# Late constants of a fused attention and mixture-of-experts kernel: one block of memsets on VectorE, or separately planned pieces

## The chip, the cores and the metric

The kernel runs on one core of one Trainium2 chip (the experiments ran in four sets, each on another such chip; a ratio always compares runs of one set). The metric is the device time of one execution in microseconds (us).

A word on names: PE is the matmul engine (TensorE), DVE is VectorE, ACT is ScalarE, POOL is GpSimd.

## The reference

Four batches of eight attention heads (768 tokens, head size 64). Every query sees its near neighbours (a band of 16 to each side) and one summary per block of 32 keys. The result x, 3072 x 512, goes through a mixture of eight experts whose weights P come from eight rounds of Sinkhorn normalization.

```python
scores_l = where(|i - j| < 16, q @ k.T / 8, -1e9)
scores_s = q @ k_blockmax.T / 8 + log(32)
a = softmax(concat([scores_l, scores_s]))
x = a @ concat([v, v_blockmean])                    # 4 batches x 8 heads
P = sinkhorn(exp(x @ w_gate - max), rounds=8)       # rows, then columns, scaled
out = sum over e of P[:, e] * (relu(x @ w1[e]) @ w2[e])
```

## The kernel before

The kernel is emitted in an order that a small planner in its own source works out. Work is cut into units; each has an engine, an estimated cost, dependencies and a rank. The planner simulates the engines with these costs and, wherever several units could start next on an engine, takes the one of lowest rank. A unit cannot be interrupted. The instructions of all engines are emitted in exactly that order, with semaphores where one engine's work needs another's.

```python
# Plan.order(), cut: for each engine, the units that could start first (within 0.02 us); among them the lowest rank
t = max([t0, free.get(e, 0.0)] + [d.end + d.lag + (HOP if d.on != e else 0.0) for d in u.deps])
best.setdefault(e, []).append((t, u, cost))
...
t_min = min(t for t, _, _ in c)
t, u, cost = min((x for x in c if x[0] <= t_min + 0.02), key=lambda x: x[1].prio)
```

Heads are worked in pairs. The four pairs of the first batch are done in two halves (h = 0, 1), so that the first expert can start on half of the tokens. The other twelve pairs are done whole, and these need some constants: zeros in E_e, zeros and ones in V_e, and col_en for the Sinkhorn stage. They are set once, after the masks of the last first-half pair.

```python
def late_constants():
    for t in E_e:
        nc.vector.memset(t[64:128, :, :], 0.0)
    for t in V_e:
        nc.vector.memset(t[:], 0.0)
        nc.vector.memset(t[0:24, :, D:VD], 32.0 / XS)
        nc.vector.memset(t[32:56, :, VD + D:2 * VD], 32.0 / XS)
    nc.vector.memset(col_en, float(E) / float(N))

# pair_half(i, h, rank), cut: masks -> value products -> normalization -> transposes -> copy into xT
U["mk", i, h] = add("DVE", 0.78, masks_h, [U["X", i, h], ...], rank)
U["ss", i, h] = add("PE", 0.22, summaries, ...)
U["A", i, h]  = add("PE", 0.65, values_h, [U["mk", i, h], U["sx", i, h], U["Vs", i]], rank)
U["no", i, h] = add("DVE", 0.68, normalize, [U["A", i, h], ...], rank)
U["xt", i, h] = add("PE", 0.18, to_xT, [U["no", i, h]], rank)
U["x", i, h]  = add({"ACT": 0.46, "DVE": 0.5}, 0, x_out, [U["xt", i, h]], rank)

# the order of building, cut
for i in range(PB):
    pair_start(i, i)
    pair_half(i, 0, i)
add("DVE", 2.4, late_constants, [U["mk", PB - 1, 0]], 5.5)
expert0(0, [U["x", i, 0] for i in range(PB)])       # first expert: hidden layer 'hps', second layer 'yps'
for i in range(PB):
    pair_half(i, 1, 10 + i)
...                                                # batches 1 to 3, the rest of expert 0
# then a "bridge" into the Sinkhorn stage, then experts 1 to 7: the main loop, whose order is fixed
```

The softmax here doesn't subtract the row's maximum and nothing guards it: scores larger than these inputs give would overflow.

## Time and profile before

Median 679.09 us of three runs (679.05 to 679.47). The profiled execution was another one: it took 684.06 us, its span was 681.4.

The first part of the page of the kernel before gives busy time, share of the span and number of instructions of each engine. The part on the chain says which engine the work that ended last ran through.

```profile
PE 670.5 (98%) x5189; PEld 441.6 (65%) x5189; DVE 585.4 (86%) x1445; ACT 407.7 (60%) x788; POOL 125.9 (18%) x165
...
PE 92%; DVE 4%; DMA 1%; issue 1%; ACT 1%; POOL 1%; DVEq 0%; ACTq 0%
```

PE is busy for 98% of the span and holds 92% of the chain. The list of waits of PE alone (who waited for whom, total us, times, longest) from 20 us to the end has only three entries:

```profile
PE sink L1077 <- DVE csum_sb L1072: 0.9, 1, 0.9
PE tx L506 <- ACT es L430: 0.6, 1, 0.6
PE sg L323 <- ACT qT L196: 0.4, 1, 0.4
```

The timeline of VectorE at the block (columns: start, duration, engine, line, operation, what is written from what, shape, count; in brackets the idle time before and what ended it):

```profile
23.50 0.78 DVE L593 MEMSET Ee<- 64x384 uint32 x2
24.41 0.38 DVE L595 MEMSET Ve<- 128x390 uint32 x1
...
25.89 0.17 DVE L598 MEMSET col_en<- 128x128 f32 x1
26.36 0.20 DVE L498 RECIPROCAL rc<-av 128x6 f32<-128x6 f32 x1 [0.30 <-PE av L468]
```

From the first memset to the end of the last: 23.50 to 26.06 us, 2.56 us. The normalization (L498 and the line after it) follows and had to wait 0.30 us more for the value products of PE. The timeline of PE there:

```profile
23.62 1.91 PE L544 MATMUL idle<-zeros 128*128 128x512 bf16 x4
25.33 0.72 PE L468 MATMUL av<-vx,Eh 128*128 128x65 bf16 x16
...
27.18 0.39 PE L323 MATMUL sg<-qT,kT 64*128 64x160 bf16 x8 [0.40 <-ACT qT L196]
...
29.04 0.33 PE L506 MATMUL tx<-ident,xs 128*128 128x128 f16 x3 [0.58 <-ACT es L430]
...
29.62 1.47 PE L200 MATMUL hps<-xT,w 128*128 128x384 f16 x8
```

The value products of the last first-half pair are "av<-vx,Eh" at 25.33; the four "idle" matmuls ahead of them are filler that the planner puts into gaps; "tx" are the transposes into xT and "hps" the first hidden-layer matmuls. In the view by stretches (length, busy us and count of each engine, granted clock, DMA) the stage looks like this:

```profile
15.28:25.52 10.24, 10.24 (x104) 6.59 (x103) 8.11 (x22) 4.60 (x7) 7.68 (x10) 0.50 1.47 195
25.52:36.00 10.48, 9.50 (x164) 6.54 (x162) 6.80 (x21) 8.08 (x14) 5.49 (x8) 1.00 1.98 172
```

The number after the POOL column is the granted clock: from 15.28 to 25.52 us PE ran at half its clock.

### The profile page before, as it was taken

How to read it: one execution, taken by the hardware profiler on the slowest of the kernel's cores; microseconds unless marked ns; L12 is line 12 of the kernel's file. 1: busy time of each engine (PE TensorE's matmuls, PEld its weight loads, DVE VectorE, ACT ScalarE, POOL GpSimd, SP SyncE). 2: the span in 40 equal slices, each digit the busy share in tenths (PEclk: the TensorE clock that was granted, in tenths of full speed). 3: DMA queues.
4: the chain of work that ended last, by engine and by line, in shares of the span. 5: the costliest groups of instructions: out<-in, count | busy, mean ns of one | idle time of the engine just before them, and what ended most of it. 6: DMA issues, size and time to landing. Idle time of an engine off the chain costs nothing.

```text
span 681.4 us, 13654 instructions
## 1 busy us (share of the span) xinstructions
PE 670.5 (98%) x5189; PEld 441.6 (65%) x5189; DVE 585.4 (86%) x1445; ACT 407.7 (60%) x788; POOL 125.9 (18%) x165
## 2 busy tenths in 40 slices
PE   8999999999999999999999999999999999999996
PEld 4665666545666666666666666666666666666665
DVE  6778898788599988999889988998899888998886
ACT  4677877656677765555555555555555555555551
POOL 8699630022202010100101010201010101100000
PEclk9799999999999999999999999999999999999999
DMA  9999990000503123310513050404131051301224
GB/s 120 188 143 143 98 144 7 1 1 0 78 1 37 12 31 48 31 17 1 78 17 33 1 78 1 48 1 60 19 31 17 7 72 17 32 1 48 78 93 155
DMA packets 113618, 33.90 MB, mean 50 GB/s; under 512 B 99984, under 2 KB 110736, under 8 KB 113552
## 3 DMA queue, kind: packets, MB, share of 16 engines
q0 software_dynamic: 104672, 26.22, 41.6%
q1 hardware_dynamic: 8352, 6.80, 3.3%
q8 instruction: 40, 0.66, 0.4%
q14 instruction: 26, 0.21, 0.1%
q10 hardware_dynamic: 528, 0.02, 0.0%
HBM read 52.45 MB, written 6.29 MB: 86 GB/s over the span
## 4 chain that ended last, share of the span: by engine, by line
PE 92%; DVE 4%; DMA 1%; issue 1%; ACT 1%; POOL 1%; DVEq 0%; ACTq 0%
PE xy L883 36%; PE pg L877 16%; PE pa L877 10%; PE pb L877 10%; PE yps L210 6%; PE hps L200 6%; PE sg L323 1%; PE tkq L304 1%; PE vs L331 1%; PE av L468 1%; PE tx L506 1%; DMA qst<-in_q_dram 1%; DVE out_acc L1018 1%; PE av L395 1%; PE av L401 1%
## 5 line engine op out<-in xcount | busy, mean ns | idle before, releaser
L883 PEld LDWEIGHTS <-hf 128*128 128x128 f16 x2352 | 230.1, 98 | 96.1 <-issue 1.2
L883 PE MATMUL xy<-w,hf 128*128 128x256 f16 x1312 | 183.4, 273 | 0.1
L883 PE MATMUL xy<-ws,hf 128*128 128x256 f16 x984 | 147.6, 273 | 0.1
L191 ACT ACTIVATE hf<-pg 128x512 f16<-128x512 f32 x84 | 50.2, 597 | 149.6 <-PE pg L877 149.4
L1018 DVE SCALAR_TENSOR_TENSOR out_acc<-xy,P_sb,out_acc 128x512 f32<-128x512 f32 x164 | 115.1, 744 | 1.7 <-PE xy L883 1.7
L824 DVE TENSOR_TENSOR hf<-hf 128x512 f16<-128x512 f16 x252 | 99.6, 422 | 8.8
L877 PE MATMUL pa<-xT,w 128*128 128x512 f16 x336 | 99.9, 379 | 0.0
L877 PEld LDWEIGHTS <-w 128*128 128x128 f16 x672 | 65.8, 98 | 43.6 <-issue 0.6
L827 DVE TENSOR_TENSOR hf<-pb,c 128x512 f16<-128x512 f32 x84 | 58.1, 692 | 38.2 <-PE pb L877 35.7
L176 POOL DMA_DIRECT2D w<-in_moe_w_dram x56 | 41.8, 759 | 220.3 <-PE pg L877 192.1
L877 PEld LDWEIGHTS <-ws 128*128 128x128 f16 x504 | 49.3, 98 | 25.3
L911 ACT COPY c<-pg 128x512 f32<-128x512 f32 x84 | 49.2, 585 | 22.7 <-PE pg L877 22.6
L827 DVE TENSOR_TENSOR hf<-pg,c 128x512 f16<-128x512 f32 x84 | 57.2, 681 | 0.6 <-PE pg L877 0.6
L191 ACT ACTIVATE hf<-pa 128x512 f16<-128x512 f32 x84 | 50.6, 603 | 0.4 <-PE pa L877 0.4
L896 ACT COPY pg<-pa 128x512 f32<-128x512 f32 x84 | 47.9, 570 | 4.8
L877 PE MATMUL pg<-xTs,w 128*128 128x512 f16 x168 | 50.0, 379 | 0.1
L877 PE MATMUL pb<-xT,ws 128*128 128x512 f16 x168 | 50.0, 379 | 0.0
L877 PE MATMUL pg<-xTs,ws 128*128 128x512 f16 x168 | 50.0, 379 | 0.0
L877 PE MATMUL pg<-xT,w 128*128 128x512 f16 x168 | 50.0, 379 | 0.0
L877 PE MATMUL pb<-xTs,ws 128*128 128x512 f16 x168 | 50.0, 379 | 0.0
L904 ACT COPY c<-pb 128x512 f32<-128x512 f32 x84 | 49.8, 593 | 0.2 <-ACT pg L896 0.2
L200 PE MATMUL hps<-xT,w 128*128 128x384 f16 x256 | 48.7, 326 | 0.0
(136 smaller groups left out, 842.5 us busy)
## 6 DMA issues: line engine op xcount, KB each, us to landing
w<-in_moe_w_dram POOLq DMA_DIRECT2D x8, 1024.0 KB, 9.3
w<-in_moe_w_dram POOLq DMA_DIRECT2D x56, 128.0 KB, 3.5
out_dram<-out_acc SPq DMA_DIRECT2D x22, 256.0 KB, 2.0
qst<-in_q_dram POOLq DMA_DIRECT2D x32, 96.0 KB, 5.8
vx<-in_v_dram POOLq DMA_DIRECT2D x16, 192.0 KB, 6.5
kst<-in_k_dram POOLq DMA_DIRECT2D x24, 96.0 KB, 6.0
w<-in_moe_w_dram POOLq DMA_DIRECT2D x2, 512.0 KB, 8.3
kst<-in_k_dram POOLq DMA_DIRECT2D x4, 192.0 KB, 4.9
```

The costliest lines, as they stand in the source:

```text
L176: nc.gpsimd.dma_start(out=t[:, :, h, :], in_=moe_w1[e].rearrange("(dk p) f -> p dk f", p=128)[:, :, f:f + 128])
L191: nc.scalar.activation(out=out, in_=in_, func=AF.Relu, bias=0.0, scale=1.0)
L200: nc.tensor.matmul(hp[:, 0:n], lhsT=w1s[e][:, dk, 128 * f:128 * (f + 1)], rhs=xT[:, dk, t0:t0 + n], start=(dk == 0), stop=(dk == KD - 1))
L210: nc.tensor.matmul(yp[:], lhsT=h[:, f, c * 128:(c + 1) * 128], rhs=w2s[e][:, f, :], start=(f == 0), stop=(f == KF - 1))
L824: nc.vector.tensor_tensor(out=out, in0=in0, in1=in1, op=ALU.subtract)
L827: nc.vector.tensor_tensor(out=out, in0=in0, in1=in1, op=ALU.add)
L877: nc.tensor.matmul(bank[:], lhsT=w[:, dk, :], rhs=x[:, dk, :], start=start and dk == 0, stop=dk == KH - 1, skip_group_check=True)
L883: nc.tensor.matmul(bank, lhsT=a(f)[:, 128 * c:128 * (c + 1)], rhs=w[:, f, :], start=start and f == 0, stop=f == FH - 1, skip_group_check=True)
L896: nc.scalar.copy(out=B["g"][:], in_=B["a"][:])
L904: nc.scalar.copy(out=B["c5"][:], in_=B["b"][:])
L911: nc.scalar.copy(out=B["c2"][:], in_=B["g"][:])
L1018: nc.vector.scalar_tensor_tensor(out=acc, in0=src, scalar=P_sb[:, t, e:e + 1], in1=acc, op0=ALU.mult, op1=ALU.add)
```

## The change

The intent: give the planner seven small units at a low rank in place of one block of 2.4 us, so that it may put more urgent VectorE work, such as the normalization, in between. (It was described as eight pieces; the code makes two for E_e, four for V_e and one for col_en.) The memsets themselves are the same nine.

```diff
         def late_constants():
-            for t in E_e:
-                nc.vector.memset(t[64:128, :, :], 0.0)
-            for t in V_e:
-                nc.vector.memset(t[:], 0.0)
+            def zero(t):
+                nc.vector.memset(t, 0.0)
+
+            def ones(t):
                 nc.vector.memset(t[0:24, :, D:VD], 32.0 / XS)
                 nc.vector.memset(t[32:56, :, VD + D:2 * VD], 32.0 / XS)
-            nc.vector.memset(col_en, float(E) / float(N))
+
+            parts = [(0.4, lambda t=t: zero(t[64:128, :, :])) for t in E_e]
+            for t in V_e:
+                parts += [(0.4, lambda t=t: zero(t[:])), (0.15, lambda t=t: ones(t))]
+            return parts + [(0.15, lambda: nc.vector.memset(col_en, float(E) / float(N)))]
...
-        add("DVE", 2.4, late_constants, [U["mk", PB - 1, 0]], 5.5)
+        c1 = U["mk", PB - 1, 0]
+        for us, fn in late_constants():
+            c1 = add("DVE", us, fn, [c1], 12.5)
```

## The prediction

> **What bounds the kernel now.** The tensor engine. The page shows PE busy 670.5 us of 681.4 (98%), and PE holds 92% of the chain that ended last. After 26 us the list of PE's waits has only three: 0.9 us for the Sinkhorn column sum (139 us), 0.6 us for an exponential's output (29.0 us) and 0.4 us for a copied query (27.2 us). The rest is matmul that this change doesn't touch, so there is little to win.
>
> **What the change does.** The same 9 memsets run on VectorE. In the timeline they are one run from 23.50 to 26.06 us: E_e 0.78, V_e 0.38 twice, four small ones 0.06 each, col_en 0.17; 2.56 us with the gaps. (The diff makes seven units of them, not eight.) Nothing is removed or added. What changes is the planner's view: instead of one 2.4 us block it has seven links of 0.15 to 0.4 us at a lower rank, so that other vector work may come between. In the plan the normalization of the last first-half pair can start about 1.2 us earlier (after three pieces, 1.2, for 2.4), and with it the transposes into xT, their copy, and the first expert's first matmuls.
>
> **What of it is critical.** On the chip the block is nearly free. From 15.3 to 25.5 us PE ran at a granted clock of 0.5 (windows view: 0.50 in 21 to 23.5). The last pair's value products therefore ran at 25.33 to 26.3, and VectorE, done with the block at 26.06, still waited 0.30 us for them. So the direct saving is about zero; after the change VectorE waits longer before that normalization, and the 1.2 us of constants left over go into its next gaps (27.15 to 28.34 is idle now). The gain can only come from PE's order after the value products: from 26.1 to 29.0 us PE is busy 1.96 of 2.90 us. If the last pair's xT is transposed earlier, the first hidden-layer matmuls (29.62 us now) can come about 1 us earlier and fill these holes. The plan is unchanged up to the block, so I expect the same first 23 us, filler matmuls and half-clock stage. Everything later is reshuffled a little, at PE full; that may win or lose some tenths of a us, also at the Sinkhorn stage.
>
> [...] I expect no second slow stage.
>
> **Prediction.** 678.4 us (0.7 less), 8 in 10 between 676.6 and 680.0. Faster by over 2%: 1%; within 2%: 98%; slower by over 2%: 1%.
>
> **What would show it.** The memsets stand in several places, mostly within 23.5 to 31 us, with a normalization between them; their busy sum stays about 2 us. The normalization still starts at 26.2 to 26.5 us and waits for PE. The first hidden-layer matmul starts at 28 to 29 us. PE's idle time between 26 and 30 us shrinks from 1.0 to under 0.5 us. PE's clock is 0.5 until 25.5 us and 1.0 after. From 30 us on the same work is shifted by under 1.5 us.
>
> **What would make it wrong.** A new order that delays a copy or mask of the second halves, so that PE waits where it is full today; constants so late that the neighbour-value transfers (first at 35.5 us) wait for them; a second half-clock window; or a Sinkhorn chain that starts later or meets the expert matmuls worse.

The sum: the median before, 679.1 us, less 0.7 for the earlier hidden layer, is 678.4.

## The result, and the profile after

| | runs | median us | range |
|---|---|---|---|
| before, first set | 4 | 679.28 | 679.05 to 679.72 |
| after, first set | 4 | 680.03 | 678.55 to 680.71 |
| before, second set | 11 | 679.58 | 679.18 to 682.60 |
| after, second set (a_copy) | 6 | 679.31 | 678.72 to 679.92 |

Ratio after to before: 1.0007 (95% interval 0.9989 to 1.0025) in the first set and 0.9990 (0.9974 to 1.0005) in the second. A ratio here is the mean time of one kernel's fast runs over that of the other's of the same rounds, so it is not quite the ratio of the medians in the table. The change moves the time by nothing that these runs can show. All outputs are right. My figure was 678.4 with a range of 676.6 to 680.0; the first median lies 0.03 us over its upper end, the second inside.

The first part of the page of after, then the list of PE's waits in after from 20 us on:

```profile
PE 667.0 (98%) x5189; PEld 438.4 (65%) x5189; DVE 583.2 (86%) x1445; ACT 406.1 (60%) x788; POOL 125.3 (18%) x165
```

```profile
PE pg L883 <- DVE xT L830: 0.8, 1, 0.8
PE ss L419 <- DVE xT L196: 0.5, 1, 0.5
PE sg L323 <- ACT qT L196: 0.4, 1, 0.4
PE tx L506 <- DVE xs L499: 0.2, 1, 0.2
```

The wait for the exponential (0.6 us, at 29.04 before) is gone, as hoped. But two new ones came, both for VectorE: 0.5 us for a copy of xT (at 70 us) and 0.8 us at the bridge into the Sinkhorn stage; the latter stands in place of the 0.9 us for the column sum. The timelines of VectorE and then of PE at the block in after, and its view by stretches:

```profile
22.23 0.79 DVE L593 MEMSET Ee<- 64x384 uint32 x2
23.14 0.38 DVE L593 MEMSET Ve<- 128x390 uint32 x1
23.56 0.20 DVE L498 RECIPROCAL rc<-av 128x6 f32<-128x6 f32 x1
...
24.62 0.38 DVE L593 MEMSET Ve<- 128x390 uint32 x1
...
25.33 0.17 DVE L602 MEMSET col_en<- 128x128 f32 x1
```

```profile
21.21 1.03 PE L544 MATMUL idle<-zeros 128*128 128x512 bf16 x4
22.08 0.64 PE L468 MATMUL av<-vx,Eh 128*128 128x65 bf16 x16
...
23.85 0.39 PE L323 MATMUL sg<-qT,kT 64*128 64x160 bf16 x8 [0.40 <-ACT qT L196]
24.40 0.34 PE L506 MATMUL tx<-ident,xs 128*128 128x128 f16 x3 [0.16 <-DVE xs L499]
24.67 0.50 PE L409 MATMUL ss<-qT,ksT 64*32 64x384 bf16 x4
...
25.56 0.82 PE L200 MATMUL hps<-xT,w 128*128 128x384 f16 x4
```

```profile
15.28:25.52 10.24, 8.55 (x152) 5.53 (x143) 8.81 (x28) 6.66 (x12) 7.53 (x10) 1.00 1.47 195
```

The order is the one that the planner was meant to find: three memsets, the normalization, six memsets; the transposes now stand ahead of the summary products "ss", and the hidden layer starts at 25.56. But everything is three microseconds earlier than in the trace of before, and that is not the change's doing. The code up to 22 us is the same in both kernels. The difference is the clock: 1.00 here, 0.50 there. The two profiles cannot be compared by their clock times. So I measure everything from one event: the start of the value products of the last first-half pair (25.33 before, 22.08 after), the last thing that is the same in all kernels (early_block below, which moves the block ahead of it, and the two with an extra ScalarE copy at the very start apart). From there to the end of the trace, before took 681.42 - 25.33 = 656.09 us, and after 678.06 - 22.08 = 655.98. I call this "the measure". Two traces of the same kernel agree in it within 0.11 us (before and b_copy, after and a_copy, plan_only and plan_only2), which is far better than the timed runs do, and it is the yardstick for the experiments. Most kernels have one trace only, so differences of about 0.1 us are not read.

### The profile page after: what moved, and what is told of

Read it like the earlier page. It is cut to its first block, busy times and chain, and to the rows that moved or that the text cites. A ratio compares the mean times of both kernels' runs of the same rounds, so it can differ in the third digit from the quotient of the medians.

```text
span 678.1 us, 13655 instructions
## 1 busy us (share of the span) xinstructions
PE 667.0 (98%) x5189; PEld 438.4 (65%) x5189; DVE 583.2 (86%) x1445; ACT 406.1 (60%) x788; POOL 125.3 (18%) x165
## 4 chain that ended last, share of the span: by engine, by line
PE 91%; DVE 5%; DMA 1%; POOL 1%; issue 1%; ACT 0%; DVEq 0%; POOLq 0%; ACTq 0%
PE xy L889 36%; PE pg L883 16%; PE pb L883 11%; PE pa L883 11%; PE yps L210 6%; PE hps L200 6%; PE tkq L304 1%; PE sg L323 1%; DMA vx<-in_v_dram 1%; DVE out_acc L1024 1%; PE vs L331 1%; PE tx L506 1%; PE av L395 1%; PE av L401 1%; PE ss L419 1%
```

## The experiments

My theory was that the change wins a few tenths at the block and that the new order behind it gives them back. The rivals: the block was never critical; or the difference lies in the clock of the runs. Numbers of all traces, in us. "To loop" is from the value products to the first second-layer matmul of the main loop ("xy"), "loop" from there to the end, and the measure is their sum (rounded each for itself).

| kernel | value products to normalization | to first "hps" | to loop | loop | measure | timed median (runs) | ratio to before |
|---|---|---|---|---|---|---|---|
| before, half clock to 25.5 | 1.03 | 4.29 | 150.99 | 505.10 | 656.09 | | |
| b_copy | 2.55 | 4.20 | 150.91 | 505.09 | 655.99 | 679.95 (6) | 1.0005 (0.9986 to 1.0023) |
| after | 1.48 | 3.48 | 151.24 | 504.74 | 655.98 | 680.03 (4) | 1.0007 (0.9989 to 1.0025) |
| a_copy | 1.43 | 3.43 | 151.21 | 504.66 | 655.87 | 679.31 (6) | 0.9990 (0.9974 to 1.0005) |
| dve_only | 1.48 | 3.58 | 150.91 | 505.10 | 656.01 | 680.53 (6) | 1.0022 (0.9997 to 1.0047) |
| plan_only | 2.74 | 4.75 | 152.52 | 504.65 | 657.18 | 682.15 (6) | 1.0030 (1.0013 to 1.0046) |
| plan_only2 | 2.74 | 4.75 | 152.51 | 504.66 | 657.17 | 683.09 (4) | 1.0041 (1.0011 to 1.0071) |
| local_only | 1.48 | 3.80 | 150.57 | 505.10 | 655.67 | 680.10 (4) | 1.0018 (0.9986 to 1.0051) |
| later_only | 2.75 | 4.19 | 151.62 | 504.66 | 656.28 | 679.63 (4) | 0.9999 (0.9978 to 1.0020) |
| early_block | 0.94 | 3.27 | 151.02 | 505.09 | 656.11 | 679.44 (4) | 1.0001 (0.9977 to 1.0025) |
| act_shift | 2.74 | 4.21 | 150.90 | 504.73 | 655.63 | 679.48 (6) | 0.9996 (0.9970 to 1.0023) |
| best | 1.48 | 3.80 | 150.56 | 504.66 | 655.23 | 679.46 (6) | 0.9990 (0.9969 to 1.0012) |
| fill | 2.75 | 4.75 | 152.51 | 504.68 | 657.19 | 680.66 (6) | 1.0005 (0.9984 to 1.0025) |
| copy_first, half clock to 25.0 | 1.17 | 3.48 | 151.26 | 504.68 | 655.94 | 680.65 (6) | 1.0007 (0.9990 to 1.0024) |

### b_copy and a_copy: the two kernels again

No edit.

> The kernel before again, for a trace at the full clock. Both theories: ratio 1.000. If the half-clock stage of the first profile (15.3 to 25.5 us, clock 0.992 over the span) belongs to the run and not to the kernel, this trace has none and its span is about 676 to 678 us. Theory 'locally won, given back later': at full clock the block of memsets (22.2 to 24.8 us) does hold up the normalization, which starts at 24.9 and not at 23.6 us as after, and the first hidden-layer matmul comes at 26.4 to 26.8 (25.56 after). Rival 'never critical': the first hidden-layer matmul starts within 0.3 us of 25.56.

> The changed kernel again: ratio 1.000 to 1.001, and its PE trace up to 36 us as in the first trace of it where the clock is the same.

In b_copy the half clock lasted 3.41 us (16.88 to 20.29), so this trace shows the block of before at full clock, here VectorE and then PE:

```profile
22.95 0.78 DVE L593 MEMSET Ee<- 64x384 uint32 x2
...
25.35 0.17 DVE L598 MEMSET col_en<- 128x128 f32 x1
25.54 0.20 DVE L498 RECIPROCAL rc<-av 128x6 f32<-128x6 f32 x1
```

```profile
23.00 0.63 PE L468 MATMUL av<-vx,Eh 128*128 128x65 bf16 x16
23.56 0.34 PE L468 MATMUL av<-Vs,es 64*128 64x130 bf16 x3
...
24.76 0.39 PE L323 MATMUL sg<-qT,kT 64*128 64x160 bf16 x8 [0.40 <-ACT qT L196]
...
26.61 0.33 PE L506 MATMUL tx<-ident,xs 128*128 128x128 f16 x3 [0.58 <-ACT es L430]
...
27.20 1.47 PE L200 MATMUL hps<-xT,w 128*128 128x384 f16 x8
```

Now VectorE is the late one: the value products end at about 23.9, and the normalization starts at 25.54, when the block is done. So the block does hold up the normalization, by about a microsecond against after (2.55 and 1.48 us behind the start of the value products). The half clock of the first profile had hidden this. What it costs PE is less: PE has other work, and its two idle stretches, 0.40 and 0.58 us, shrink to 0.40 and 0.16 after. Nor is it the late normalization alone that holds PE here: the profile puts the end of the 0.58 us down to ScalarE's exponential "es" (its first one ends at 26.57 us, the normalization at 26.33). In the trace of before the normalization was done 1.89 us ahead of the transposes "tx", and yet these stood 3.71 us behind the start of the value products, here 3.61. In dve_only below the same transposes start 2.98 us behind it and ahead of that exponential. How the order of VectorE brings the wait for the exponential about is not shown. The trace was not free of the stage and the span not 676 to 678 us, as I had hoped, and so the normalization and "hps" stand 0.4 to 0.8 us later by the clock than expected; relative to the value products the expectation of the first theory holds. The stage is also shorter than in the first trace of the same code (10.24 us): it belongs to the run and not to the kernel. a_copy showed no half clock, and its normalization and first "hps" stand as in the first trace of after; the ratio was 0.9990, just below the 1.000 to 1.001 expected.

### dve_only and plan_only: the two halves of the change apart

dve_only keeps the plan of before and moves only the memsets on VectorE; plan_only keeps the plan of after and puts the memsets back in one block.

```diff
# dve_only, against before
 def late_constants():                       # still one unit of 2.4 us in the plan
-    ...all nine memsets
+    ...E_e, E_e, V_e[0]; the other six go to a list
 def normalize(i, h):
     ...
+    while (i, h) == (PB - 1, 0) and rest:
+        rest.pop(0)()                       # behind the normalization of the last first-half pair
# plan_only, against after
-for us, fn in late_constants():
-    c1 = add("DVE", us, fn, [c1], 12.5)
+parts = late_constants()                    # same seven units in the plan; the first emits all nine memsets
+for n, (us, _) in enumerate(parts):
+    c1 = add("DVE", us, (lambda: [fn() for _, fn in parts]) if n == 0 else (lambda: None), [c1], 12.5)
```

> The order of all engines as before (planned with one block of 2.4 us), but on VectorE the normalization of the last first-half pair stands ahead of the last six memsets. If the block on the chip is what costs: the normalization starts at about 23.6 us and the time is 0.5 to 1.2 us shorter than before. If only the later order matters: same as before within 0.3 us.

> The order of all engines as after (planned in seven pieces), but the nine memsets stand in one block ahead of the normalization. If the block on the chip is what costs: 0.5 to 1.2 us longer than after, with a new wait of PE for the normalization (before the transposes into xT) near 24.5 to 25.5 us. If only the later order matters: same as after within 0.3 us.

plan_only shows what the block can cost (the timeline of PE). Its PE order asks for the transposes early, and they must wait for a normalization that stands behind the block:

```profile
23.77 0.39 PE L323 MATMUL sg<-qT,kT 64*128 64x160 bf16 x8 [0.41 <-ACT qT L196]
25.59 0.34 PE L506 MATMUL tx<-ident,xs 128*128 128x128 f16 x3 [1.42 <-DVE xs L499]
```

The line of 25.59 shows 1.42 us of idle PE ahead of the transposes, ended by the normalization ("xs"), and the measure is 1.20 us longer than after's 655.98, all of it still there at the end: what was lost at the block was not won back. dve_only, in turn, won 0.6 us up to the first "hps" and yet ended with the measure of before, which is the outcome "only the later order matters". Its trace shows where the gain went. At the first-layer matmuls just ahead of the transposes of pair 4's keys it was still 0.33 us ahead of b_copy (11.46 and 11.79 us behind the start of the value products), exactly where local_only below stands. Then the second of the two transfers of these keys landed 12.55 us after its issue, at 34.26 us (in b_copy 11.00 us after it, at 32.63), and the transposes of the keys started at 34.40 us, 0.34 us later behind those matmuls than in b_copy. (The profile names a copy of ScalarE for this wait, but in b_copy and local_only the same transposes start before that copy ends.) So a late transfer took the gain away. The edit doesn't touch this transfer, and no other trace was held up there; with one trace of dve_only, its measure decides nothing. The timed runs of plan_only were also slower than its trace explains, by more than a microsecond; more of that below.

### local_only, later_only, early_block: the block against everything behind it

local_only has the plan of before, with the order at the block (VectorE, and PE's transposes) made as after by hand. later_only has the plan of after, with the order at the block made as before. early_block moves the whole block to the start of the kernel.

```diff
# local_only, against dve_only
+for key in (("no", 3, 0), ("xt", 3, 0), ("x", 3, 0)):
+    place(U[key], ahead_of=U["ss", 0, 1])
# later_only, against plan_only
+for key in (("xt", 3, 0), ("x", 3, 0), ("S", 1, 1), ("X", 1, 1)):
+    place(U[key], ahead_of=U["hd", 0, 0])
# early_block, against before
-add("DVE", 2.4, late_constants, [U["mk", PB - 1, 0]], 5.5)
+add("DVE", 2.4, late_constants, [U["ident"]], -4.0)
```

> Planned as before (one block), and then by hand at the block only: the normalization ahead of the last six memsets, and the transposes and copy of the last first-half pair ahead of the summary products, as after has them. All other order is that of before. Measured from the start of the last pair's value products to the end of the trace, where the first 22 us (same code in all kernels) drop out: before 656.0 to 656.1 us, after 655.9 to 656.0. If the change wins locally and its later order gives the win back: 655.4 to 655.8. If the local order wins nothing that lasts: 655.9 to 656.2. In the timed runs under 0.2% either way.

> Planned as after (seven pieces), and then by hand at the block only: all nine memsets in one block ahead of the normalization, and the transposes, their copy and the next score products as before has them; the later order is that of after. Same measure. If the local order is worth about 0.3 us and the later order gives it back: 656.2 to 656.5. If the local order is worth nothing: 655.9 to 656.1.

> Before, with the whole block planned right behind the identity matrix (about 5.3 to 7.9 us) instead of at 22 us, so nothing stands between the value products and the normalization. If the block still costs something after the change: the normalization starts within 0.3 us of the end of its value products, and the measure from those products to the end is 655.2 to 655.8; the start may be up to 0.9 us later. If no place of the block matters: 655.9 to 656.2.

The two-by-two table of the measure comes out additive:

| measure, us | later order of before | later order of after |
|---|---|---|
| block as before | 655.99 (b_copy) | 656.28 (later_only) |
| block as after | 655.67 (local_only) | 655.98 (after) |

The order at the block (VectorE's and PE's together) is worth 0.32 us with the one later order and 0.30 with the other; act_shift and best below repeat the pair, with 0.40. The later order of after costs 0.29 and 0.31. The two cancel. The theory "won at the block, given back later" stands in the traces, and the rival "never critical" falls. The third, the clock of the runs, explains the spread of the timed runs: of the 46 runs of the code of before whose clock is on record, the 35 with a mean clock of 0.998 or more had spans of 677.0 to 678.6 us, the 8 with 0.995 or less 679.0 to 681.7. It also explains the look of the first profile, but hardly the measure: the half-clock stages reach only 0.19 us (before) and 0.59 us (copy_first) into it. (Both first traces also end at a clock of 0.5, before in its last 0.5 us and after in its last 0.2, but PE's last matmul has ended 5.5 us before the end in before and 5.6 in after.) The later cost has two parts with opposite signs, though: up to the main loop the later order of after loses 0.71 and 0.67 us (150.91 to 151.62, 150.57 to 151.24), and in the main loop it gains 0.43 and 0.36 (505.09 to 504.66, 505.10 to 504.74). The second is odd, because the order of the main loop is fixed and the same in all kernels.

The first is not what the list of waits suggests. The view by stretches from the value products to the loop, for b_copy, later_only, local_only and after (PE's busy time is the number behind the first comma):

```profile
23.00:173.91 150.91, 148.67 (x1491) 89.36 (x1490) 122.73 (x326) 105.29 (x178) 66.44 (x83) 1.00 0.99 75
21.68:173.30 151.62, 149.37 (x1491) 88.77 (x1491) 121.39 (x327) 103.78 (x178) 66.48 (x84) 1.00 0.98 76
21.62:172.19 150.57, 148.76 (x1490) 89.20 (x1490) 122.56 (x327) 105.20 (x178) 67.51 (x84) 1.00 0.99 77
22.08:173.32 151.24, 149.37 (x1490) 88.70 (x1490) 121.09 (x327) 103.90 (x178) 66.71 (x84) 1.00 0.99 75
```

PE is idle for 2.24 and 2.25 us with the block as before, for 1.81 and 1.87 us with the block as after: the order at the block wins 0.4 us of idle time, and the later order loses next to none. Its new waits (0.5 and 0.8 us) only take the place of others. Its loss of 0.71 and 0.67 us is nearly all in time in which PE is recorded as busy, 0.70 and 0.61 us more for as many matmuls. The profile's page says of itself that the ends of matmuls are modelled, so short stalls may hide in this time; whether they do, and what they are, is not shown.

early_block is the best at the block: the normalization follows the value products at once, and "hps" starts 0.2 us earlier than after. Its measure, 656.11, is that of before all the same: this is the outcome "no place of the block matters". But its own plan has a new later order too, with the same two later waits as after, so it is no clean test of the block. Against after it is 0.22 us shorter up to the loop (151.02 and 151.24) and 0.35 longer in it (505.09 and 504.74), and the second belongs to the effect of the next section. The start was not delayed either (value products at 21.63 us). The 0.2 to 0.8 us that I expected if the block still cost something are not there. In the timed runs none of these three differs from before.

### act_shift, best: the 0.4 us in the main loop

In traces with a loop of 505.1 us, PE is about 0.2 us late twice with a second-layer matmul, at 34.5 and 259.6 us behind the start of the loop; in the others it isn't. In both places ScalarE starts one copy ("c<-pg") 0.28 us later than in the other traces, although PE's product that it reads stands at the same time behind the start of the loop in both, and the two copies are 384 recorded ScalarE instructions apart. In every trace where the first of these copies is late, 319 recorded ScalarE instructions stand ahead of it, those that only wait for a semaphore or issue a transfer counted (before, b_copy, dve_only, local_only, early_block); where it is on time there are 320 (after, a_copy, the plan_only kernels) or 318 (later_only). The new plan swaps some copies and other work between ScalarE and VectorE, but as many of ScalarE's computing instructions stand ahead of the copy in after as in before (244); the number differs by one semaphore instruction. early_block has nearly the ScalarE work of after, but 319, and is late. So I shifted ScalarE's instruction stream by one:

```diff
# act_shift, against before; best, against local_only
 nc.scalar.activation(out=warm[:], in_=warm[:], func=AF.Exp, bias=0.0, scale=1.0)
+nc.scalar.copy(out=warm[:], in_=warm[:])     # 8 numbers, at the start, where ScalarE is idle
```

> Before, with one extra ScalarE copy of 8 numbers right at the start, so that every later ScalarE instruction has a number one higher. In all traces with the later order of before, ScalarE starts one copy 0.28 us late at two places of the main loop, 384 of its instructions apart, and PE loses 0.21 us at each; the traces with the later order of after, whose numbers are shifted by one or whose instruction there is another, do not. If it hangs on the number in the instruction stream: from the first second-layer matmul to the end 504.66 us instead of 505.10, and from the value products to the end 655.55 to 655.7. If it hangs on what the plan left behind on VectorE or in the buffers: 505.10 again.

> local_only and that extra copy: the local order of after, the later order of before, no late ScalarE copies. If both effects stand and add up: 655.2 to 655.3 us from the value products to the end, the shortest of all, 0.7 to 0.8 less than before and after. In the timed runs 0.1% at most, inside their spread. If the shift does nothing: 655.67 again.

The timelines of ScalarE, then of PE, at the first of the two places in b_copy:

```profile
207.00 0.59 ACT L911 COPY c<-pg 128x512 f32<-128x512 f32 x1 [0.56 <-PE pg L877]
```

```profile
207.77 0.59 PE L877 MATMUL pg<-xT,w 128*128 128x512 f16 x2
208.42 0.60 PE L883 MATMUL xy<-w,hf 128*128 128x256 f16 x4
```

The same instructions in act_shift:

```profile
205.44 0.58 ACT L912 COPY c<-pg 128x512 f32<-128x512 f32 x1 [0.28 <-PE pg L878]
```

```profile
206.49 0.59 PE L878 MATMUL pg<-xT,w 128*128 128x512 f16 x2
206.92 0.60 PE L884 MATMUL xy<-w,hf 128*128 128x256 f16 x4
```

The idle time of ScalarE ahead of the copy falls from 0.56 to 0.28 us, and the step from "pg" to "xy" on PE from 0.65 to 0.43. Loop: 504.73 instead of 505.09. In all 14 traces (act_shift and best have 320) the copy is late exactly where 319 instructions stand ahead of it, and one extra instruction, far away and without any use, puts it on time. So this part of the gain is not a merit of the change's order: it hangs on where an instruction stands in ScalarE's stream, or on something else that shifts with it, which was not tested apart. Why ScalarE is late there stays open; no record in the trace names it.

best puts local_only and the shift together: 655.23, the shortest measure, 0.76 us below before and 0.75 below after, as the sum of the two effects (655.99 - 0.32 - 0.36 = 655.31, an estimate from b_copy, local_only and act_shift) asks. In the timed runs it is 0.9990 of before, interval 0.9969 to 1.0012: not told apart from it.

### plan_only2 and fill: times that the trace does not explain

```diff
# fill, against plan_only
+if u is U["xt", PB - 1, 0]:
+    keep_busy(4)                            # four filler matmuls where PE stalls 1.4 us
```

> plan_only again. Its trace lost 1.2 us against after, its timed runs 2.8. If the block alone costs 1.2 us and the rest is half-clock windows that its longer stall of PE (1.4 us) brings on, another profile may show a window of 0.5 after 24 us, and the time is 681 to 683 us again. If the rest was chance: 680 to 681 us.

> plan_only with four filler matmuls in the stall of PE (1.4 us) ahead of the transposes; at full clock they take 0.86 us and fit in. The trace should not change: 657.1 to 657.3 from the value products to the end. If the timed runs of plan_only are 2.8 to 3.8 us slower, and not 1.2, because its stall brings on half-clock windows: now 680.3 to 681 us. If it is something else: 682 to 684 again.

plan_only2 is plan_only once more: the trace is the same within 0.01 us, again without a half-clock stage, and the timed runs are slow again (680.30, 683.71, 682.47, 683.89). With the filler the trace stays the same too (657.19), but the times fall to 679.99 to 681.15, which is what 1.2 us on top of before predicts. So 1.6 and 2.8 us of plan_only's loss (medians, each over the before of its own set) went away with four filler matmuls in the stall. (In the trace of plan_only, at a clock of 1.00, PE's next matmul starts 0.86 us behind the first of four such, at 22.00 and 21.14 us: the figure of the expectation.) That fits half-clock stages in the unprofiled runs. No kept trace of plan_only caught one, but the record has the mean clock of every timed run: 0.995 or 0.996 in the five unprofiled runs of plan_only and 0.993 to 0.996 in the three of plan_only2, against 0.998 in the two profiled ones, and 0.998 to 1.000 in all six runs of fill. So the slow runs did run at a lower clock, and with the filler none did. That the stall itself brings the lower clock on was my guess; these clocks fit it, no trace shows it. Where in these runs the half clock lay is not shown either.

### copy_first: the wait at 70 us

The wait that after shows at 70 us stands in the traces of after, a_copy, later_only, plan_only, fill and early_block, and in none with the later order of before. VectorE does a mask there before the copy that frees the buffer. So I took the copy first:

```diff
# copy_first, against after
+seq.remove(U["x", 7])
+seq.insert(seq.index(U["mk", 8, 0]), U["x", 7])
```

> After, with one change of order on VectorE at 69 us: the copy of pair 7 into xT ahead of the mask of pair 8, so that the buffer for which PE waits 0.50 us at 70.06 us (in every trace with the later order of after, in none of before) comes free 0.5 us sooner. All else is the order of after. If that wait is most of the 0.67 us that the later order costs ahead of the main loop: from the value products to the first second-layer matmul 150.6 to 150.8 us instead of 151.2, and to the end 655.3 to 655.5. If the mask, now later, makes PE wait as long, or the gain is lost at the Sinkhorn stage: 151.1 to 151.3 and 655.9 to 656.0.

The timeline of PE in after, then in copy_first, where the summary products stand:

```profile
70.06 0.65 PE L419 MATMUL ss<-qT,ksT 64*32 64x384 bf16 x4 [0.50 <-DVE xT L196]
```

```profile
72.17 0.34 PE L419 MATMUL ss<-qT,ksT 64*32 64x384 bf16 x2 [0.31 <-DVE xT L196]
72.67 0.34 PE L419 MATMUL ss<-qT,ksT 64*32 64x384 bf16 x2 [0.16 <-ACT kT L196]
```

The 0.50 us became 0.31 and 0.16: freed sooner from VectorE, PE waited for ScalarE instead. The measure is unchanged, 655.94. The second of the two outcomes came, so the 0.67 us that the later order costs ahead of the loop are not this one wait. That agrees with the view by stretches above, where PE's idle time did not grow.

This trace has a half-clock stage of 6.83 us (view by stretches), so kernels with the plan of after have them as well:

```profile
18.14:24.97 6.83, 6.83 (x68) 4.11 (x64) 4.88 (x13) 3.04 (x6) 5.36 (x7) 0.50 1.36 201
```

## Why the prediction was right or wrong, point by point

- **PE bounds the kernel, there is little to win.** Right. By the medians all kernels lie within 0.2% of the before of their set, but for plan_only (0.4 and 0.6%).
- **The same memsets, nothing added; the plan unchanged up to the block; the normalization after three pieces.** Right. 1445 VectorE instructions in both, the planned order as foreseen, filler and all up to 22 us alike.
- **"On the chip the block is nearly free." The direct saving is about zero.** Wrong as put. I read it from a profile taken in a half-clock run, where PE was so slow that VectorE was done with the block first. At full clock the block holds the normalization (2.55 us behind the start of the value products; 1.48 after), and the order at the block is worth 0.30 to 0.32 us. That the late normalization is the whole way to this cost is not shown: in the order of before PE's wait ends with ScalarE's exponential.
- **"The normalization still starts at 26.2 to 26.5 us and waits for PE."** Wrong: at full clock it starts at 23.56 us, and it is VectorE's third memset that ends just before it.
- **The first hidden-layer matmuls about 1 us earlier; PE's idle time from 1.0 to under 0.5 us.** Nearly: 0.72 us earlier behind the value products (4.20 to 3.48), and the idle time from 0.98 to 0.56 us. The mechanism is right: the transposes come earlier and the hidden layer fills the hole. But of the 0.7 us in my figure this gave only 0.30 to 0.32.
- **Everything later is reshuffled; that "may win or lose some tenths of a us".** This is the other mis-sized term. I let it be zero in my sum, and it measured a loss of 0.29 to 0.31 us: 0.67 to 0.71 lost ahead of the main loop, nearly all while PE is recorded as busy, and 0.36 to 0.43 won in it, a gain that one extra ScalarE copy brings as well (0.36 in act_shift). With 0.3 won at the block, 0.7 in all became 0.0 to 0.2 in the traces (656.09 and 655.99 against 655.98 and 655.87).
- **The same half-clock stage, and no second one.** The wrong question. What the traces show is two clocks, 0.50 and 1.00. In the 3.41 us ahead of the drop PE was busy for 2.00 us in before, 1.95 in copy_first and 2.29 in b_copy, but 2.00 us in plan_only (24.05 to 27.47 us) and 1.98 in plan_only2 (23.33 to 26.74) were followed by no drop. Throughout the half clock PE was recorded as busy (3.41 of 3.41 us in b_copy, 6.83 of 6.83 in copy_first, 10.24 of 10.24 in before), so in these traces PE's busy time over such a stretch alone tells neither when the clock falls nor when it comes back. The trace of after had no such stage up to the end of PE's work. The stages last 3.41, 6.83 and 10.24 us, so two and three times the shortest, and they fall differently in runs of the same code: from 15.28 us in before, from 16.88 in b_copy. They explain most of the slow runs among the profiled ones: the value products began at 23.00, 24.37 and 25.33 us in the traces with a stage of 3.41, 6.83 and 10.24 us, and at 21.41 to 22.08 us in those without, so a stage cost less than half its length (at most 1.59, 2.96 and 3.92 us against the earliest of those without). The profiled runs with such a stage took 681.48, 682.76 and 684.06 us, and the ones without (plan_only and its variants apart) 679.05 to 679.76. A part of that lies outside the span of the trace (2.5 to 2.6 us there, 1.7 to 2.1 in the others), and the traces don't say why.

What stays open: why ScalarE is late at two places, why PE is busy 0.6 to 0.7 us longer with the later order, how the block's order makes PE wait for the exponential, and what exactly brings on a half-clock stage. No timed run shows any of these few tenths: they are read from traces alone.

## What to carry to other kernels

Before reading a profile, look whether the clock in it is the clock of the runs that were timed: a trace from a disturbed run can show a critical block as idle-covered (here, at a clock of 0.50, the normalization came 1.03 us behind the start of the value products and waited for PE; at full clock it came 2.55 us behind it, when the block was done). When a planner orders everything, a local edit reshuffles all that follows, so test the edit and the new order apart, by replaying one order with the other's local piece, and measure from an event behind which the kernels first differ. An effect of a few tenths of a microsecond may have nothing to do with the work of the change (here one extra ScalarE copy at the start took 0.36 us off the main loop). And before a list of waits is taken for the cause, compare the engine's idle time in sum: here new waits came, and the idle time stayed the same.
